# Multi-query attention beside a gated MLP on one core: scores, exponentials and P·V replaced by key moments of third order, under a new list scheduler

## The chip, the cores and the metric

The kernel runs on one core of a Trainium2 chip. The core has a matrix engine (PE, with weight loads listed as PEld), a vector engine (DVE), a scalar engine (ACT), a general engine (POOL), and a sync engine (SP) that mostly issues DMAs; 16 DMA engines move data. Matrix results land in PSUM, eight banks of 128 x 512 float32. Every engine executes its own instruction stream strictly in order and waits on semaphores that other engines raise. The metric is device time of one launch in microseconds, as the median of several runs; a profile is one execution with its own span.

## The reference

```
x = A_x                                    # 2048 x 512, bf16
g = sigmoid((x * gate_w).sum(-1))
q = (x @ wq) -> 32 heads of 16;  k = x @ wk;  v = x @ wv      # one k and v for all heads
p = softmax(q k^T / 4);  a = (p v, heads joined) @ wo
z = gelu(x @ w_in)                         # 2048 x 1376, two halves of 688
z2 = layernorm(second half);  gg = w_sp @ z2 + b_sp           # w_sp is 2048 x 2048
b = (first half * gg) @ w_out
out = g * a + (1 - g) * b
```

All inputs are normal numbers times 0.1 (w_sp times a further 0.01). The scores are small: worked out from the reference's own inputs in float32, the largest |q|² of a head is 2.934, the largest |k/4|² is 0.1369, and the largest score is 0.383.

## The kernel before

Attention is done in 32 units, each 512 queries (one of four chunks) times four heads. For a unit there are 16 key tiles x 4 heads = 64 score blocks of 128 keys by 512 queries. PE makes them (`s_mm`, `ps<-QA,KA`; every matmul goes through the helper at line 394 with a tile position, so that four matmuls on 32 rows or 32 columns of the array run side by side; four such are called a quad below). The blocks are then divided between two ways to exp:

- ACT takes the exp of two or three blocks at a time out of PSUM into a ring `P` (`exp_op`, line 830).
- DVE takes other blocks through a range-checked polynomial: line 842 reads PSUM and writes a linear form into `UW`, line 850 squares it, line 856 squares it again, on DVE or on POOL. The constant and linear rests of the polynomial come back as sums over keys (`SVB`, `KTV`).

PE multiplies the results with `V` into bank 7 (`ps<-P,V` and `ps<-UW,V`). A column of ones in `V` gives the denominators; DVE transposes the unit's result (line 868), and POOL normalises it. The check of the range (`good`, line 920) ends in a flag; were it set, a general path would do all of it again after the fast one.

Beside that run the projections (`xT,wqd`), the second half of z with its normalisation (lines 646 to 670), the first half (lines 639 and 1431), the product with w_sp (`ps<-wT,z`, 24 groups of 17 quads, times the first half at line 714), and the output products (`wo,OT` and `wout,z`, lines 788 and 790).

The order of the instructions on every engine is written by a planner in the build (`pe_step`, `act_step`, `dve_step`, `pool_step`), which keeps a clock per engine with written-out costs. It also puts in products with zeros, `ps<-CT,zer`, where PE's recent share of work in its plan falls below a set value. SP's queue carries few transfers: transposing loads of x, `wT<-in_B_w_sp` in four rounds of four, the weights and the outputs.

Of the kernel before, what the change touches and what calls it, by code (L numbers as in the profile page):

```python
# [2 lines left out]

# [4 lines left out]
ALU = mybir.AluOpType  # L8
# [51 lines left out]
ZP = ()  # L60
W_WIN = 3400.0
W_GEL = 0.98
PR = dict(HALF=100.0, IDR=10, IDN=4, WRES=18, D_HG=3600.0, D_FL=False, WIN=1000.0, WIH=560.0, BACK=32, PRESS=4, FLEX=5000.0, RMIN=48, WBL=0.4, W_MIN=0.9, TTR=50.0, PMX=4, WMX=900.0, PTO=6000.0, PSL=80.0, WP0=45000.0, WG=0, HOLD=0.0, RLEND=0, BMH=2600.0, FST=0.0, TFE=740000.0, PMG=100.0, PLR=130.0)
SCHED = {}
HINT = dict(pe=200, act=40, dve=110, pool=40)
NCHK = 16
L_PE = 235.0
L_X = 40.0
D_END = 110.0
D_DEP = 117.0  # L70
C_SW = 103.0
INFO = None

# [15 lines left out]
class Prog:  # L89

    ENG = ("pe", "act", "dve", "pool", "sp")

    def __init__(self, name):
        self.name = name
        self.ops = {e: [] for e in self.ENG}
        self.lastw = {}
        self.readers = {}
        self.ndma = 0  # L100
# [1934 lines left out]
```

## Time and profile before

| what | value |
|---|---|
| median of 3 runs | 721.99 us (721.9 to 722.15) |
| profiled execution, span | 719.4 us |
| PE busy, matmuls | 700.0 us, 8732 |
| DVE busy, instructions | 702.9 us, 992 |
| ACT busy, instructions | 702.3 us, 752 |
| POOL busy, instructions | 533.9 us, 463 |
| exps on ACT (line 830) | 677.1 us |
| DMA moved | 20.04 MB, mean 28 GB/s |

The median of the runs is 2.6 us above the profile's span; the span is from the first to the last instruction of one execution. Busy time on PE counts a matmul until its modelled end, so that two pipelined matmuls overlap in it; how far apart matmuls start says more. The granted PE clock is shown as a share of full speed.

### The profile page before, as it was taken

The page shows a single profiled execution, that of the slowest core. Times are in us where ns is not written, and L with a number is a line of the kernel's source. Part 1 is how long each engine was busy: PE and PEld are TensorE (multiplying, and loading weights), DVE is VectorE, ACT ScalarE, POOL GpSimd, SP SyncE. Part 2 cuts the span into 40 slices and gives each one's busy share as a digit, 9 for nine tenths or more (in the row PEclk, how much of TensorE's full clock was granted, in tenths as well). Part 3 has the DMA queues.
Part 4 walks back from the last instruction along what each step waited for, and adds up shares of the span by engine and source line. Part 5 has one row for each costly group of instructions (what it writes and reads, how often), then busy time and mean ns, then how long its engine had stood idle before and what let it go on. Part 6 is the DMA issues. An engine that isn't in the chain of part 4 may idle for free. (4 is left out here: it accounts for less than half of the span.)

```text
span 719.4 us, 21284 instructions
## 1 busy us (share of the span) xinstructions
PE 700.0 (97%) x8732; PEld 205.8 (29%) x8732; DVE 702.9 (98%) x992; ACT 702.3 (98%) x752; POOL 533.9 (74%) x463
## 2 busy tenths in 40 slices
PE   8999999999999999999999999999999999999997
PEld 3322223322522222222222322222322222223222
DVE  5999999999999999999999999999999999999997
ACT  5999999999999999999999999999999999999995
POOL 5358877877546857888777888787887787777882
PEclk9999999999999999999999999999999999999999
DMA  8334000000001000510002340000052000000000
GB/s 162 110 94 89 2 1 2 2 3 1 3 1 31 2 1 2 104 43 4 3 1 39 61 81 9 3 1 2 2 118 31 1 17 17 1 2 2 18 14 32
DMA packets 59804, 20.04 MB, mean 28 GB/s; under 512 B 54804, under 2 KB 59192, under 8 KB 59704
## 3 DMA queue, kind: packets, MB, share of 16 engines
q1 hardware_dynamic: 57448, 18.36, 12.1%
q8 instruction: 69, 1.13, 0.7%
q10 hardware_dynamic: 2256, 0.30, 0.3%
q14 instruction: 31, 0.25, 0.1%
HBM read 3.38 MB, written 2.10 MB: 8 GB/s over the span
## 5 line engine op out<-in xcount | busy, mean ns | idle before, releaser
L830 ACT ACTIVATE P<-ps 128x1024 bf16<-128x1024 f32 (+1 forms) x732 | 677.1, 1104 | 2.4 <-PE ps L394 1.8
L856 POOL TENSOR_TENSOR UW<-UW 128x512 f16<-128x512 f16 (+3 forms) x341 | 441.3, 1294 | 128.9 <-DVE UW L842 44.3
L842 DVE TENSOR_SCALAR UW<-ps 128x512 f16<-128x512 f32 (+1 forms) x433 | 359.2, 853 | 3.4 <-PE ps L394 1.8
L394 PE MATMUL ps<-QA,KA 32*128 32x512 bf16 x2048 | 316.3, 384 | 11.2 <-ACT P L830 5.1
L394 PE MATMUL ps<-P,V 128*32 128x512 bf16 x1472 | 184.9, 386 | 0.4 <-DVE KN L563 0.2
L850 DVE TENSOR_TENSOR UW<-UW 128x2048 f16<-128x2048 f16 (+1 forms) x154 | 179.4, 1165 | 0.4
L394 PEld LDWEIGHTS ps<-QA,KA 32*128 32x128 bf16 x2048 | 82.4, 91 | 303.3 <-ACT P L830 146.6
L394 PE MATMUL ps<-wT,z 128*32 128x512 bf16 (+1 forms) x1536 | 111.5, 366 | 0.0
L394 PE MATMUL ps<-UW,V 128*32 128x512 f16 x576 | 108.1, 384 | 0.3
L856 DVE TENSOR_TENSOR UW<-UW 128x1024 f16<-128x1024 f16 (+6 forms) x147 | 96.6, 671 | 0.0
L394 PEld LDWEIGHTS ps<-P,V 128*32 128x32 bf16 x1472 | 43.5, 94 | 61.6 <-issue 57.9
L394 PEld LDWEIGHTS ps<-wT,z 128*32 128x32 bf16 x1536 | 27.8, 94 | 43.3 <-issue 40.0
L394 PE MATMUL ps<-CT,zer 128*32 128x512 bf16 x416 | 37.1, 383 | 0.0
L539 POOL TENSOR_TENSOR QSQ<-QA 128x512 bf16<-128x512 bf16 x16 | 24.8, 1552 | 13.8 <-DVE UW L842 5.7
L394 PEld LDWEIGHTS ps<-UW,V 128*32 128x32 bf16 x576 | 25.4, 94 | 19.0 <-issue 12.0
L394 PE MATMUL ps<-wout,z 128*32 128x512 bf16 x384 | 30.3, 384 | 0.1
L394 PE MATMUL ps<-win,xT 128*32 128x344 bf16 x512 | 29.5, 313 | 0.2 <-DVE z L646 0.2
L868 DVE STREAM_TRANSPOSE T<-ps 128x512 f32<-128x512 f32 (+1 forms) x33 | 22.6, 688 | 0.7 <-PE ps L394 0.7
L394 PE MATMUL ps<-CT,SVB 128*32 128x512 bf16 x128 | 22.8, 383 | 0.0
L394 PE MATMUL ps<-xT,win 128*32 128x512 bf16 (+1 forms) x384 | 22.1, 363 | 0.1
L394 PE MATMUL ps<-xT,wqd 128*32 128x512 bf16 x256 | 21.9, 386 | 0.1
L896 POOL TENSOR_TENSOR win<-T,rc 128x512 bf16<-128x512 f32 x11 | 17.6, 1600 | 3.9 <-DVE UW L856 2.6
(111 smaller groups left out, 329.3 us busy)
## 6 DMA issues: line engine op xcount, KB each, us to landing
out_dram<-outsb SPq DMA_DIRECT2D x15, 128.0 KB, 1.9
win<-in_B_w_in_dram SPq DMA_DIRECT2D x1, 1376.0 KB, 6.3
wout<-in_B_w_out_dram SPq DMA_DIRECT2D x1, 640.0 KB, 4.1
wo<-in_A_wo_dram SPq DMA_DIRECT2D x8, 64.0 KB, 2.4
KA<-KA SPq DMA_DIRECT2D x4, 112.0 KB, 2.4
UW<-in_A_wq_dram SPq DMA_DIRECT2D x1, 384.0 KB, 4.1
wT<-in_B_w_sp_dram SPq DMA_TRANSPOSE x16, 4.5
UW<-in_A_wq_dram ACTq DMA_DIRECT2D x1, 128.0 KB, 3.9
```

The costliest lines, as they stand in the source:

```text
L394: return t.matmul(dst, lhsT, rhs, start=start, stop=stop, tile_position=tp)
L539: dq(pl_q, 1050.0, lambda: op("pool", lambda v: v.tensor_tensor(QSQ[:, q % 2, :], QA[:, q % NQ, :], QA[:, q % NQ, :], ALU.mult), r=[("Q", ...
L830: op("act", lambda a: a.activation(P[:, 512 * p0:512 * (p0 + n)], ps[:, 512 * b0:512 * (b0 + n)], ACT.Exp), r=[bkey(b0 + i_) for i_ in ran ...
L842: op("dve", lambda v: v.tensor_scalar(UW[:, s, 512 * i:512 * (i + n)], bank(b, 512 * n), Q_A, Q_AS, ALU.mult, ALU.add), r=[bkey(b + j) for ...
L850: op("dve", lambda v: v.tensor_tensor(src, src, src, ALU.mult), r=k, w=k, tag="dTT")
L856: op(eng, lambda v: v.tensor_tensor(src, src, src, ALU.mult), r=[("U", s, h) for h in range(a // 2, (b + 1) // 2)], w=w, after=after, tag= ...
L868: return lambda: pgx.op("dve", lambda v: v.transpose(T1[:, jj, c0:c1], bank(BO, c1 - c0, c0)), r=[bkey(BO)], w=[("T1", jj, c0)], tag="T1")
L896: pgx.op(eng, lambda v: v.tensor_tensor(dst, t1v[:, j0:j1, b0:b1, 0:16], rc[:, j0:j1, b0:b1].unsqueeze(3).broadcast_to([128, n, nb, 16]), ...
```

## The change

The scores are no longer formed. Exp is replaced by a cubic, C0 + C1 s + C2 s² + C3 s³, valid for |s| up to 0.655. Since s is a product of q and k, sums over keys can be taken first:

- **Moments (once).** From k and v the kernel forms sums over all 2048 keys of v, k, k kᵀ (as pairs), and of pair products of k times k and times v (`K3`, `T`; lines 549 to 588). The pairs are k_r k_(r+i) for r = 0..15 and i = 0..7, so 128 rows; i = 8 is handled apart (`E`, `kkE`).
- **Pair products of queries.** Work goes in 16 units of 512 queries x 8 heads, each in two halves of four heads. `Qt` is written to DRAM (`qe`, line 618; eight wrapped rows are copied behind it, line 620) and read back in two layouts: `Y` repeats each dimension r eight times, `YB` gives dimension r+i (lines 628 and 630, 512 KB each), and `E` reads pairs for i = 8. `X = Y * YB` is 128 x 512 per head (line 658, on DVE or POOL, as the planner chose).
- **Meeting the moments.** For every head two quads make `W = T3ᵀ X`, 256 x 512, in a pair of banks, (0,1) or (2,3). DVE multiplies both by the query (`Pr`, line 665, 128 x 1024 out of PSUM), and a quad with a 0/1 matrix (`Pr,cs`) sums over the dimension into the numerator bank 4. Lower orders are added there by `T1b`, `TEb`, `M2`; the denominators are gathered in bank 5 (`T2b`, `T3d`), and DVE finishes them at line 680.
- **Per 512 queries (line 691 on).** Denominators of four units are joined, inverted, spread by 0/1 products (`Rh,sg`), and line 702 writes the normalised heads into `OT`, which lies in the buffer of `win`.
- **The MLP** is the same mathematics. Both gelus now read PSUM on ACT (lines 712, 738), with quads as before.
- **The range check** compares max |q|² · max |k/4|² with 0.655² / 1.016 = 0.4223; the flag leads to a general path that computes scores, maxima and exps.
- **The planner** is new: a list scheduler (`Plan.run`) over tasks with costs and priorities; it deals out banks (0 to 3 for `W` while it lasts, 4 and 5 for a unit's sums, 6 and 7 for the rest) and takes for each engine the ready task of lowest priority number. It has no filling with zeros; 11 warming matmuls of 128 columns stand at the start.

Cut to its core, the diff is:

```diff
-        def s_mm(dst_bank, blk, key):
-            u, kt, g = blk
-            e = u % 2
-            kr = ["K0a" if kt == 4 * XO[0] else ("K0", kt // 4)] if e == 0 else [("K1", kt // 4)]
-            mm(bank(dst_bank), KA[32 * g:32 * g + 32, e, 128 * kt:128 * kt + 128], QA[32 * g:32 * g + 32, (u // 2) % NQ, :], True, True,
-               kr + [("Q", (u // 2) % NQ)], [key], tp=(32 * g, 0), chan="s", tag="S")
...
-            op("act", lambda a: a.activation(P[:, 512 * p0:512 * (p0 + n)], ps[:, 512 * b0:512 * (b0 + n)], ACT.Exp),
-               r=[bkey(b0 + i_) for i_ in range(n)], w=[("P", p0 + i_) for i_ in range(n)], tag="exp")
...
-            op("dve", lambda v: v.tensor_scalar(UW[:, s, 512 * i:512 * (i + n)], bank(b, 512 * n), Q_A, Q_AS, ALU.mult, ALU.add),
...
+        def g_q(u):
+            tg, G = u // 4, u % 4
+            s = u % NQT
+            g = Group("any")
...
+            add({"act": (520.0, lambda a: a.activation(Qt[:, s, :], bank(g.b), ACT.Copy))}, 0, None, w=[("Q", s)], grp=g, evac=True, pri=1, tag="Qev")
+            o0 = 24 * 4096 * u
+
+            def wr(q):
+                return [q.dma_start(dap(qe, o0 + 512 * j, [[2048, 2], [4096, 16], [1, 512]]), Qt[32 * j:32 * j + 32, s, :]) for j in range(4)]
...
+            load("sp", lambda q: q.dma_start(Y[:, n % NY, :, :].rearrange("p j n -> p (j n)"), dap(qe, o0, [[4096, 16], [0, 8], [1, 2048]])), [("Y", n % NY)], r=[("qe", u)],
+                 size=524288, pri=10 + u + 0.1 * e, chan="y%d" % (n % NY), tag="Y")
...
+                    xf = lambda v, xi=xi, j=j, n=n: v.tensor_tensor(X[:, xi, :], Y[:, n % NY, j, :], YB[:, n % NYB, j, :], ALU.mult)
+                    add({"pool": (1350.0, xf), "dve": (370.0, xf)}, 0, None,
+                        r=[("Y", n % NY), ("YB", n % NYB)], w=[("X", xi)], pri=pr_, tag="X")
+                    gw = Group("W", 2)
+                    for t in range(2):
+                        add("pe", c_mm(512), mm4(lambda gw=gw, t=t: gw.b + t, 512, 0, T3[:, t, :], X[:, xi, :], True, True),
+                            r=["T3", ("X", xi)], grp=gw, pri=pr_, tag="W")
+                    add("dve", 1150.0, lambda v, gw=gw, pi=pi, n=n, j=j: v.tensor_tensor(Pr[:, pi, :, :], bank(gw.b, 1024).rearrange("p (t n) -> p t n", t=2),
+                                                                                      Y[:, n % NY, j, :].unsqueeze(1).broadcast_to([128, 2, 512]), ALU.mult),
+                        r=[("Y", n % NY)], w=[("Pr", pi)], grp=gw, evac=True, pri=5, tag="Pr")
...
+        def allowed(g, plan):
+            k = g.banks
+            if k == "W":
+                return (0, 2)
+            if k in ("N", "T"):
+                return (4,)
+            if k in ("D", "K3"):
+                return (5,)
...
+        add("dve", 80.0, lambda v: v.tensor_scalar(qk1[0:32, 5:6], qk1[0:32, 2:3], S_MAX * S_MAX / SLACK, None, ALU.is_le), r=["qk2"], w=["qk4"], pri=30, tag="guard")
```

How the streams change is best seen in three places. SP's queue at the start, first before, then now (`L301` and `L507` load x, `L618` writes `Qt` to DRAM, `L620` copies the wrapped rows, `L628` and `L630` load `Y` and `YB`):

```order
L301 DMA_TRANSPOSE xT<-in_A_x_dram 128x4x512 x2
L305 DMA UW<-in_A_wq_dram 128x4x384
L301 DMA_TRANSPOSE xT<-in_A_x_dram 128x4x512 x2
L313 DMA KA<-KA 112x512 x3
L319 DMA win<-in_B_w_in_dram 128x4x1376
```

```order
L507 DMA_TRANSPOSE xT<-in_A_x_dram 128x4x512 x4
L618 DMA qe<-Qt 2x16x512 x16
L620 DMA qe<-qe 16x2048
L628 DMA Y<-qe 128x1x2048
L644 DMA E<-qe 128x512
L628 DMA Y<-qe 128x1x2048
L620 DMA qe<-qe 16x2048
L630 DMA YB<-qe 128x1x2048
```

Sixteen small writes now stand between the loads of x and the first `Y` and `YB`, where three copies of keys stood.

DVE in the middle of attention, first before, then now (`Pr` is the product out of a bank pair, `X` the pair product, `z` at `L767` the MLP's gating, `win` at `L702` the buffer that holds `OT`):

```order
L842 TENSOR_SCALAR UW<-ps 128x1024
L856 TENSOR_TENSOR UW<-UW 128x768
L850 TENSOR_TENSOR UW<-UW 128x2048
L842 TENSOR_SCALAR UW<-ps 128x1024
L856 TENSOR_TENSOR UW<-UW 128x1024
```

```order
L658 TENSOR_TENSOR X<-Y,YB 128x512 x2
L702 SCALAR_TENSOR_TENSOR win<-Ns,S,ps 128x512
L665 TENSOR_TENSOR Pr<-ps,Y 128x1024
L702 SCALAR_TENSOR_TENSOR win<-Ns,S,ps 128x512
L680 SCALAR_TENSOR_TENSOR Prd<-ps,T1d,Qt 128x512
L767 TENSOR_TENSOR z<-ps,z 128x512
L702 SCALAR_TENSOR_TENSOR win<-Ns,S,ps 128x512
L665 TENSOR_TENSOR Pr<-ps,Y 128x1024
```

Most of DVE's work still comes out of PSUM, but between two `Pr` stand single pieces of other work.

PE near its end (`Prd,cs` joins the last denominators, `wT,z` is the product with w_sp, `wo,win` and `wout,z` the output products):

```order
L469 MATMUL ps<-X,T 32x512 x8
L728 MATMUL ps<-wT,z 32x256 x32
L469 MATMUL ps<-bspz,ones 32x512 x4
L469 MATMUL ps<-wT,z 32x512 x12
L476 MATMUL ps<-Prd,cs 32x128 x16
L469 MATMUL ps<-wT,z 32x512 x16
L476 MATMUL ps<-Pr,cs 32x512 x8
L469 MATMUL ps<-wo,win 32x512 x16
L469 MATMUL ps<-wout,z 32x512 x8
```

```order
L469 MATMUL ps<-bspz,ones 32x512 x4
L469 MATMUL ps<-wT,z 32x512 x16
L469 MATMUL ps<-wout,z 32x512 x16
L469 MATMUL ps<-wT,z 32x512 x48
L728 MATMUL ps<-bspz,ones 32x256 x4
L728 MATMUL ps<-wT,z 32x256 x36
L469 MATMUL ps<-wout,z 32x512 x16
L728 MATMUL ps<-wT,z 32x256 x28
L469 MATMUL ps<-wout,z 32x512 x16
```

The last `W` is the first row of the first piece; behind the last denominators, PE still has most of the fourth round of the w_sp product and eight output tiles, and the second piece ends its stream. Before, that work stood among score blocks.

By count of these streams the changed kernel's PE issues 1076 quads of 512 columns, 128 of 344, 84 of 256, 16 of 288, 176 of 128 columns and 112 smaller; DVE some 380 instructions, of them 128 `Pr` and 42 `X`; POOL 86 `X` and 16 `E`; ACT 120 activations; SP 221 transfers.

More of the change, by code (lines that the diff above doesn't have):

```diff
@@ L287, in build_kernel, with diag, mm4, f @@
-        dprev = [None]
-        def sp_dma(fn, r=(), w=(), n=16, chain=True, tag=""):
-            o = op("sp", fn, r=r, w=w, dma=n, after=[dprev[0]] if chain and dprev[0] is not None else [], tag=tag)
-            dprev[0] = o
-            return o
+        def diag(t):
+            a = t[:, :, :]
+            return bass.AP(tensor=a.tensor, offset=a.offset, ap=[a.ap[0], [48, 2], [1, 16]])
+        pl = Plan()
+        pl.bank_last = [None] * 8
+        add = pl.add
+        def mm4(b, n, off, lhsT, rhs, start, stop):
+            def f(t):
+                return [t.matmul(ps[32 * q:32 * q + 32, 512 * b() + off:512 * b() + off + n], lhsT[:, 32 * q:32 * q + 32], rhs,
+                                 start=start, stop=stop, tile_position=(0, 32 * q)) for q in range(4)]
+            return f
@@ L294, in nonc, with load @@
+        def load(eng, fn, w, r=(), size=0, n=1, pri=0.0, chan=None, rate=DMA_RATE, tag="", after=()):
+            if chan is None:
+                chan = "d%d" % nd[0]
+                nd[0] += 1
+            return add(eng, 2600.0 if rate < DMA_RATE else 540.0 * n, fn, r=r, w=w, dma=16 * n, size=size, pri=pri, chan=chan, rate=rate, tag=tag, after=after)
         def nonc(fn):
@@ new lines, in build_kernel @@
+        gw_ = Group("any")
+        for _ in range(WARM):
+            add("pe", 430.0, lambda t: t.matmul(bank(gw_.b, 128), ones[:], ones[:], start=True, stop=True), r=["ones"], grp=gw_, pri=-1, tag="warm")
+        add("dve", 100.0, lambda v: v.tensor_copy(qk1[:, 7:8], bank(gw_.b, 1)), w=["junk"], grp=gw_, evac=True, pri=0)
+        for c in range(4):
+            load("sp", lambda q, c=c: q.dma_start_transpose(xT[:, :, 512 * c:512 * c + 512], x2[512 * c:512 * c + 512, :]), [("x", c)],
+                 size=524288, pri=c, rate=187.0, tag="x")
@@ L724, in put_out @@
[L724 to L725 removed]
+                return [t.matmul(ps[32 * q:32 * q + 32, 512 * b() + off:512 * b() + off + 256], lhsT[:, 32 * (q % 2):32 * (q % 2) + 32], rhs[:, 256 * (q // 2):256 * (q // 2) + 256],
+                                 start=start, stop=stop, tile_position=(0, 32 * q)) for q in range(4)]
+            return f
@@ L1012, in build_kernel @@
-        st_ = {"ua": 0, "kf": 0, "ke": 0, "pu": 0, "gate": False, "mode": "P", "nact": None, "run": 0}
-        stepb = {}
-        sdone = {}
-        estart = {}
-        eend = {-1: 0.0, -2: 0.0}
-        pbusy_ = [False] * PB
-        pfree_ = [0.0] * PB
-        ppos = [0]
-        def p_alloc(n, now):
-            p0 = ppos[0] if ppos[0] + n <= PB else 0
-            if any(pbusy_[i] or pfree_[i] > now for i in range(p0, p0 + n)):
-                return None
-            return p0
-        pr = dict(PR, **SCHED.get(0, {}))
@@ new lines, in build_kernel @@
+        first_w = [t for t in pl.tasks if t.tag == "mom"][0]
+        def allowed(g, plan):
[6 more added lines that the diff above has]
+                return (5,)
+            wide = first_w.eng is None or last_w.eng is not None
+            if k == "L":
+                return (0, 1, 2, 3) if last_w.eng is not None else ()
+            if k == "any" and wide:
+                return (6, 7, 0, 1, 2, 3)
+            return (6, 7)
```

2387 lines of the change are left out of this document (754 added, 1633 removed).

## The prediction

> **What bounds the kernel now.** First the page's busy shares and the costliest groups.
>
> ```profile
> span 719.4 us, 21284 instructions
> PE 700.0 (97%) x8732; PEld 205.8 (29%) x8732; DVE 702.9 (98%) x992; ACT 702.3 (98%) x752; POOL 533.9 (74%) x463
> ```
>
> ACT and DVE are both full; the groups kept apart by shape say with what:
>
> ```profile
> L830 ACT ACTIVATE P<-ps 128x1024 bf16<-128x1024 f32 x722 | 665.9, 1100 | 1.4 <-PE ps L394 0.9
> L842 DVE TENSOR_SCALAR UW<-ps 128x512 f16<-128x512 f32 x290 | 187.2, 677 | 2.9 <-PE ps L394 1.4
> L842 DVE TENSOR_SCALAR UW<-ps 128x1024 f16<-128x1024 f32 x143 | 173.1, 1211 | 0.6 <-PE ps L394 0.4
> ```
>
> ACT spends 666 us of 719 on exps of two score blocks, and idles 1.4 us before them. DVE takes the blocks that ACT cannot. So the number of scores to put through exp on two engines sets the time. That work goes away altogether; what bounds the new kernel has to be built up from its parts.
>
> **What one piece of work costs.** The start-to-start distance in a dense stretch is the price, since neighbours overlap. From the timeline:
>
> ```profile
> 404.67 1.21 DVE L842 TENSOR_SCALAR UW<-ps 128x1024 f16<-128x1024 f32 x1
> 405.80 0.67 DVE L856 TENSOR_TENSOR UW<-UW 128x1024 f16<-128x1024 f16 x1
> 406.40 0.68 DVE L535 CAST QA<-ps 128x512 bf16<-128x512 f32 x1
> 407.00 1.27 DVE L842 TENSOR_SCALAR UW<-ps 128x512 f16<-128x512 f32 x2
> 403.21 0.40 DVE L714 TENSOR_TENSOR z<-ps,z 112x256 bf16<-112x256 f32 x1
> 403.55 1.20 DVE L850 TENSOR_TENSOR UW<-UW 128x2048 f16<-128x2048 f16 x1
> ```
>
> 1024 columns out of PSUM take 1.13 us (404.67 to 405.80), 512 take 0.60, and 256 with a second tensor from SBUF 0.34: the second tensor adds nothing, so a `Pr` costs 1.13 when dense. Each DVE instruction is 0.07 to 0.08 us cheaper than its own duration. If overlap fails because every `Pr` waits for PE, the price is the whole 1.21.
>
> ```profile
> 185.23 3.41 PE L394 MATMUL ps<-xT,win 128*32 128x512 bf16 x60
> 11.58 0.70 PE L394 MATMUL ps<-wvg,xT 128*32 128x33 bf16 x64
> ```
>
> 60 matmuls are 15 quads: (3.41 - 0.38) / 14 = 0.216 us per quad of 512 columns, 0.38 being the length of one (3.41 us covers 15 starts and one end). 16 small quads take 0.70 us, 0.044 each. Other widths lie between in proportion: 0.146 for 344 columns, 0.109 for 256, 0.12 for 288, 0.056 for 128.
>
> **PE.** 1076 x 0.216 = 232.8; 128 x 0.146 = 18.7; 84 x 0.109 = 9.2; 16 x 0.12 = 2.0; 176 x 0.056 = 9.9; 112 x 0.044 = 4.9; together 277.5 us. Along PE's stream 22.6 us of this stands ahead of the first `W`, 216 from there to the last denominators, 39 behind them.
>
> **DVE.** Durations from these rows, less 0.075 each:
>
> ```profile
> L856 DVE TENSOR_TENSOR UW<-UW 128x512 f16<-128x512 f16 x17 | 7.0, 412 | 0.0
> L714 DVE TENSOR_TENSOR z<-ps,z 128x512 bf16<-128x512 f32 x20 | 13.5, 677 | 0.0
> L760 DVE SCALAR_TENSOR_TENSOR outsb<-ps,G,z 128x512 bf16<-128x512 f32 x2 | 1.4, 748 | 0.2 <-PE ps L394 0.2
> L660 DVE BATCH_NORM_STATS2 bst<-z 128x6 f32<-128x344 bf16 x32 | 13.8, 495 | 0.0
> L670 DVE TENSOR_SCALAR z<-z,mv,rstd 128x688 bf16<-128x688 bf16 x16 | 8.0, 568 | 0.0
> L517 DVE TENSOR_REDUCE km<-ps 128x1 f32<-128x512 f32 x4 | 2.7, 666 | 0.0
> L881 DVE RECIPROCAL rc<-T 128x32 f32<-128x32 f32 x15 | 5.0, 330 | 0.0
> ```
>
> 128 `Pr` x 1.136 = 145.4; 42 `X` x 0.337 = 14.2; 32 at lines 680 and 702 x 0.673 = 21.5; 20 gatings x 0.602 = 12.0; 32 statistics x 0.42 = 13.4; 16 normalisations x 0.493 = 7.9; 16 maxima of 128 columns at 0.2 = 3.2 (from the 512-column reduction, 384 columns less); four inversions of 128 columns at 1.05 (330 ns at 32, eight ns per further column) and their neighbours, 7; moments, projections' copies and the rest some 17. Together about 241 us; by full durations 269. Some 21 us stand ahead of the first `Pr`, 210 between it and the last denominators, 9 behind.
>
> So neither engine is clear of the other: between first `W` and last denominators PE has 216 us, DVE 210 (232 if nothing overlaps). Taking the eight stretches of 16 `W` and the larger of the two in each gives 219. PE has the last word, since 39 us of its work stand behind the last denominators, where DVE has 9.
>
> **ACT and POOL** fall out of the bound. ACT: 120 activations at 0.59 us or less:
>
> ```profile
> L830 ACT ACTIVATE P<-ps 128x512 bf16<-128x512 f32 x1 | 0.6, 592 | 0.0
> 18.32 1.22 DVE L842 TENSOR_SCALAR UW<-ps 128x1024 f16<-128x1024 f32 x1
> 18.48 1.04 POOL L539 TENSOR_TENSOR QSQ<-QA 128x512 bf16<-128x512 bf16 x1 [2.31 <-DVE UW L850]
> L539 POOL TENSOR_TENSOR QSQ<-QA 128x512 bf16<-128x512 bf16 x16 | 24.8, 1552 | 13.8 <-DVE UW L842 5.7
> ```
>
> about 71 us with four table loads. POOL: 106 products, 1.04 us beside a DVE that reads PSUM, 1.55 in the mean of the old mix; 110 to 165 us, hidden under 216.
>
> **The start.**
>
> ```profile
> 0.72 5.04 SPq L301 DMA_TRANSPOSE xT<-in_A_x_dram  x2
> 32.51 5.04 SPq L325 DMA_DIRECT2D wo<-in_A_wo_dram  x8
> wout<-in_B_w_out_dram SPq DMA_DIRECT2D x1, 640.0 KB, 4.1
> xT<-in_A_x_dram SPq DMA_TRANSPOSE x4, 5.5
> ```
>
> SP issues a transposing load in 2.52 us and a plain one in 0.63. Four of the first end at 10.8; sixteen writes of `Qt` take 10.1 more, to 20.9; six further issues bring the first `YB` to 24.7, and it lands 4.1 us from its issue (the 640 KB row; these are 512 KB), at 28. One product on DVE later, PE can start `W` at about 29. The moments are not later: the last chunk of x is issued at 8.3 and lands 5.5 later, at 14 (at 17 if the weights slow it), and projection, pair products, the sums and their copies add some 6 to 8 us on DVE. PE itself has 22.6 us of work from 6.2 on, part of it at a cold clock, which also ends near 29. I take 29.
>
> **The end.**
>
> ```profile
> 713.62 0.82 PE L394 MATMUL ps<-win 128*32 128x512 bf16 x11
> 714.27 1.26 ACT L788 ACTIVATE outsb<-ps,G 128x512 bf16<-128x512 f32 x2 [4.24 <-PE ps L394]
> 714.62 2.29 SPq L725 DMA_DIRECT2D out_dram<-outsb  x3
> ```
>
> From PE's last end (714.4) to the end of the span (719.4) are 5.0 us: two evictions, the store, its landing. The new end is the same.
>
> **The sum.** 29 to the first `W`, 255 of PE's work from there, 5.0 at the end: 289 with PE never waiting. Waits between the two nearly equal engines are not in any row. They cost nothing if one always hides the other; 3 if only the eight stretches count (219 for 216); 16 if DVE's full durations pace the middle (232 for 216); and 11 where a `W` stands behind a stretch of about 5 us of other work, which the stream has four times (a fifth, of 12.6 us, falls where DVE has the statistics to do), while DVE has at most two `Pr` in hand (2.3 us): 4 x 2.7 = 11. I take 13, between the last two. That is a span of 302, and with 2.6 for what the median (721.99) has over the span, **305 us**; the forecast's own range is 294 to 325. Against 722 it is 417 us less.
>
> **Cover that could fail.** The traffic is new: a unit loads 2.1 MB of `Y` and `YB`, 0.26 of `E`, moves 0.2 through `qe` and 0.13 out, and has on average one transposing load of w_sp.
>
> ```profile
> 21.00:24.00 3.00, 2.92 (x89) 1.50 (x84) 3.00 (x5) 3.00 (x5) 1.66 (x2) 1.00 1.01 400
> 48.00:66.00 18.00, 17.66 (x209) 5.16 (x208) 17.90 (x26) 18.00 (x20) 14.47 (x12) 1.00 0.56 117
> ```
>
> (The last three columns are granted clock, share of the DMA engines, GB/s.) The load of `win` went at 400 GB/s; the four transposing loads of w_sp kept the engines 0.56 x 18 = 10.1 us, 2.5 each. A unit then needs 2.69 / 0.4 + 2.5 = 9.2 us of DMA against 216 / 16 = 13.5 on PE: hidden, with a third to spare. SP issues some 13 transfers per unit, about 10 us: hidden too, but in one queue, in which a `Y` stands behind waits of `Qt` writes and w_sp loads.
>
> **Rivals.**
>
> *DMA paces the middle (17 in 100).* If rows of 1 and 4 KB out of DRAM go at half the rate of `win`, a unit needs 13.4 + 2.5 = 16 us: 16 x 16 = 256 for 216, so with half the forecast's waits 302 + 40 - 6 + 2.6, about **340 us**. For it: no row shows reads of written DRAM. Against: 400 GB/s with rows of 2.75 KB. It decides once a unit's DMA is over 13.5 us. The Trainium skill, page "DMA: Bandwidth & Descriptors", section "Why a DMA increments its semaphore by 16 and not by 1", says that a transfer uses as many engines as divide both slowest dimensions; the `Qt` writes, whose slowest dimension is 2, would use two, and no run here shows such a transfer. By its 27 GiB/s per engine I estimate 2.3 us more per unit on those two: not over 13.5 by itself.
>
> *The clock falls (9 in 100).* The new planner does not fill PE's gaps, and
>
> ```profile
> 9.00:12.00 3.00, 2.25 (x94) 1.02 (x82) 0.49 (x3) 2.94 (x3) 1.78 (x5) 1.00 1.37 237
> 716.00:718.00 2.00, 0.00 (x0) 0.00 (x0) 0.00 (x0) 0.00 (x0) 0.00 (x0) 0.63 0.58 193
> ```
>
> PE at 2.25 of 3 us keeps clock 1.00; without work it falls to 0.63 and then lower. If a quarter of PE's clock is lost from the first `W` on, 255 becomes 340, and the waits vanish in it: 29 + 340 + 5 + 3 = **377 us**. It decides where PE's share falls well under three quarters; the sum gives 277.5 of 302. The Trainium skill, "TensorE: Matmul & The Clock Gate", section "A second HAM failure mode: psum-queue depth-cycling", speaks against this change: PE that idles briefly between groups while it cycles through PSUM banks can drop to half clock again and again. The trace agrees only that idleness drops it, here to 0.63.
>
> *The range check says no (2 in 100): slower than before.* Then the general path follows the fast one: 32 passes of 16 key tiles, each with two exps of 1024 (1.10 us each by line 830) and, in a first sweep, maxima over 2048 columns (2.26 by twice 1.13): 32 x 16 x 4.46 = 2284 us, about **2,590 us** in all. It decides at 0.4223; the inputs give 2.934 x 0.1369 = 0.4017, five per cent under, more than bf16 rounding of squares takes. This is also the case in which the change doesn't do what it says.
>
> *The forecast: 72 in 100.*
>
> **How the numbers follow.** Within 0.2% of 722 (about what a measurement of this kernel can tell from no change) no case falls; only the refused range check is slower. Faster 0.98, same 0, slower 0.02. The range for 8 in 10 reaches from the forecast's low end past its high end into the DMA case: 294 to 345. The clock case is left out.
>
> **What would show it.** Right: PE and DVE both at 80 to 92% busy with neither ACT nor POOL above 60%; the first `W` at 27 to 31 us; some 40 us from the last denominators to the end with DVE nearly idle; `Pr` at 1.1 to 1.2 us; the chain of waits mostly PE. Wrong: `Pr` over 1.3 us, or starts of quads over 0.23 us; the first `W` after 35; idle time before `X` put down to `Y` or `YB` (DMA); a granted clock under 0.95 (clock gate); a busy ACT behind the end (general path).

## The result and the profile after

The changed kernel takes **344.2 us** in the median of five runs (342.3 to 350.3) against 721.9 before: a ratio of 0.4752, 95% interval 0.474 to 0.4763. The forecast was 305 us with a range of 294 to 345. The time lies just inside the range's upper end, 39 us above the point.

The profiled execution of the changed kernel is one of its slower ones (span 348.4 us, granted clock 0.973 over the span; the other four spans were 340.5 to 345.8). First the heads of the page and the groups that the prediction priced:

```profile
span 348.4 us, 14091 instructions
PE 300.0 (86%) x6381; PEld 165.7 (48%) x6381; DVE 267.8 (77%) x381; ACT 69.5 (20%) x124; POOL 132.8 (38%) x125
L665 DVE TENSOR_TENSOR Pr<-ps,Y 128x1024 bf16<-128x1024 f32 x128 | 150.9, 1213 | 8.8 <-PE ps L469 7.2
L658 POOL TENSOR_TENSOR X<-Y,YB 128x512 bf16<-128x512 bf16 x86 | 101.1, 1176 | 100.3 <-DMA YB<-qe 57.5
L658 DVE TENSOR_TENSOR X<-Y,YB 128x512 bf16<-128x512 bf16 x42 | 29.3, 736 | 5.1 <-DMA YB<-qe 3.2
YB<-qe SPq DMA_DIRECT2D x32, 512.0 KB, 6.7
```

PE is busy for 86% of the span and DVE for 77%; neither ACT nor POOL comes near the bound. The price of a `Pr` is as forecast. Three rows are not: an `X` on DVE takes 0.736 us where 0.412 was taken, POOL waits 57.5 us for `YB`, and a load of `YB` lands 6.7 us after its issue instead of 4.1.

The span in three stretches, cut at the first `W` and at the last denominators (the start of line 691's last instruction). The columns are length, busy time of PE, PEld, DVE, ACT and POOL, granted clock, share of the DMA engines and GB/s:

```profile
0.00:50.38 50.38, 30.14 (x927) 20.56 (x931) 27.27 (x67) 17.45 (x31) 15.77 (x25) 0.89 0.79 169
50.38:304.00 253.62, 231.17 (x4623) 123.22 (x4618) 230.34 (x299) 47.39 (x87) 117.07 (x101) 0.99 0.89 192
304.00:348.40 44.40, 38.73 (x840) 21.93 (x832) 10.22 (x18) 4.62 (x7) 0.00 (x0) 0.98 0.09 28
```

The forecast had 29, 229 (216 of work and 13 of waits) and 44 (39 and 5.0). So the start is 21 us longer, the middle 25, and the end is right. In the middle the DMA engines are taken for 0.89 of the time, which the forecast put at two thirds (9.2 of 13.5 us).

The chain of waits, in order of time, shows what a late `YB` does there (start, length, what; this chain reaches back to 135 us):

```profile
150.24 5.43 DMA YB<-qe
...
167.83 4.84 SPq L746
...
172.78 0.53 SPq L628
...
173.41 7.26 DMA YB<-qe
...
250.03 6.72 DMA YB<-qe
```

Three times the chain leaves PE and DVE and runs through a load of `YB`; at 167.83 SP's transposing load of w_sp (line 746) stands in front of it as well. And the start, by the timeline:

```profile
0.73 19.91 SPq L507 DMA_TRANSPOSE xT<-in_A_x_dram  x4
20.69 10.05 SPq L618 DMA_DIRECT2D qe<-Qt  x16
34.28 0.51 SPq L630 DMA_DIRECT2D YB<-qe  x1
40.29 1.15 PE L469 MATMUL ps<-wT 128*32 128x288 bf16 x15 [3.58 <-issue]
41.55 0.42 DVE L574 TENSOR_TENSOR T<-ps,cf 128x256 bf16<-128x256 f32 x1 [3.87 <-PE ps L469]
42.94 1.01 POOL L719 TENSOR_TENSOR rstd<-ve,nhalf 128x4 f32<-128x4 f32 x1 [8.26 <-DVE ve L718]
44.01 4.29 DVE L722 TENSOR_SCALAR z<-z,mv,rstd 128x688 bf16<-128x688 bf16 x4
44.19 1.29 POOL L658 TENSOR_TENSOR X<-Y,YB 128x512 bf16<-128x512 bf16 x1 [0.23 <-POOL rstd L719]
48.98 1.62 PE L469 MATMUL ps<-win,xT 128*32 128x344 bf16 x20 [4.50 <-DVE qm L816]
50.38 1.92 PE L469 MATMUL ps<-X,T 128*32 128x512 bf16 x16
52.17 1.12 DVE L603 TENSOR_SCALAR G<-gs 128x16 f32<-128x16 f32 x1
```

The loads of x keep SP until 20.6 us, not 10.8. The sixteen writes of `Qt` then take the 10.1 us that were forecast. The third moment is written at 41.6 (`T`, line 574), and 9 us pass from there to the first `W`: one group of PE waits for `qm`, which stands on DVE behind four normalisations of 1.07 us each.

### The profile page after: what moved, and what is told of

Same layout as the page of the kernel before. It is cut to its first block, busy times and chain, and to the rows that moved or that the text cites. A ratio compares the mean times of both kernels' runs of the same rounds, so it can differ in the third digit from the quotient of the medians.

```text
span 348.4 us, 14091 instructions
## 1 busy us (share of the span) xinstructions
PE 300.0 (86%) x6381; PEld 165.7 (48%) x6381; DVE 267.8 (77%) x381; ACT 69.5 (20%) x124; POOL 132.8 (38%) x125
## 4 chain that ended last, share of the span: by engine, by line
PE 39%; DVE 9%; DMA 6%; issue 3%; SPq 2%; POOL 1%; DVEq 0%; POOLq 0%
PE ps L469 32%; DMA YB<-qe 6%; PE ps L476 4%; DVE Pr L665 4%; DVE X L658 3%; PE ps L728 2%; SPq L746 1%; POOL X L658 1%; DVE win L702 1%; DVE Prd L680 0%; DVE outsb L794 0%; SPq L628 0%; DVE Rf L692 0%; DVE Rf L693 0%; SPq L796 0%
## 5 line engine op out<-in xcount | busy, mean ns | idle before, releaser
L665 DVE TENSOR_TENSOR Pr<-ps,Y 128x1024 bf16<-128x1024 f32 x128 | 150.9, 1213 | 8.8 <-PE ps L469 7.2
L658 POOL TENSOR_TENSOR X<-Y,YB 128x512 bf16<-128x512 bf16 x86 | 101.1, 1176 | 100.3 <-DMA YB<-qe 57.5
L469 PE MATMUL ps<-X,T 128*32 128x512 bf16 x1024 | 83.4, 388 | 11.3 <-issue 3.7
L469 PE MATMUL ps<-wT,z 128*32 128x512 bf16 x1280 | 88.5, 380 | 2.2 <-issue 2.2
L469 PEld LDWEIGHTS ps<-X,T 128*32 128x32 bf16 x1024 | 28.3, 97 | 40.9 <-DVE Pr L665 12.8
L767 DVE TENSOR_TENSOR z<-ps,z 128x512 bf16<-128x512 f32 x20 | 13.6, 680 | 29.1 <-PE ps L469 29.1
L658 DVE TENSOR_TENSOR X<-Y,YB 128x512 bf16<-128x512 bf16 x42 | 29.3, 736 | 5.1 <-DMA YB<-qe 3.2
L646 POOL TENSOR_TENSOR E<-E 128x512 bf16<-128x512 bf16 x16 | 18.5, 1158 | 22.7 <-DMA E<-qe 21.2
L476 PE MATMUL ps<-Pr,cs 128*32 128x512 bf16 x256 | 21.6, 388 | 2.0 <-DVE Pr L665 1.9
L714 DVE BATCH_NORM_STATS2 bst<-z 128x6 f32<-128x344 bf16 x32 | 15.1, 493 | 9.1 <-ACT z L712 9.1
L469 PE MATMUL ps<-xT,win 128*32 128x512 bf16 x320 | 20.8, 380 | 0.0
L469 PE MATMUL ps<-xT,wq 128*32 128x512 bf16 x256 | 18.5, 398 | 0.7 <-DMA wq<-in_A_wq_dram 0.5
L702 DVE SCALAR_TENSOR_TENSOR win<-Ns,S,ps 128x512 bf16<-128x512 f32 x16 | 11.7, 741 | 6.8 <-PE ps L469 6.2
```

The costliest lines, as they stand in the source:

```text
L469: return [t.matmul(ps[32 * q:32 * q + 32, 512 * b() + off:512 * b() + off + n], lhsT[:, 32 * q:32 * q + 32], rhs, start=start, stop=stop, ...
L476: return [t.matmul(ps[32 * q:32 * q + 32, 512 * b() + off:512 * b() + off + n], lhsTs[q], rhss[q], start=start, stop=stop, tile_position=( ...
L646: add("pool", 1350.0, lambda v: v.tensor_tensor(E[:, 1, u % 2, :], E[:, 1, u % 2, :], E[:, 0, u % 2, :], ALU.mult), r=[("E", 0, u % 2)], w ...
L658: xf = lambda v, xi=xi, j=j, n=n: v.tensor_tensor(X[:, xi, :], Y[:, n % NY, j, :], YB[:, n % NYB, j, :], ALU.mult)
L665: add("dve", 1150.0, lambda v, gw=gw, pi=pi, n=n, j=j: v.tensor_tensor(Pr[:, pi, :, :], bank(gw.b, 1024).rearrange("p (t n) -> p t n", t=2 ...
L702: add("dve", 640.0, lambda v, gr=gr, u=u, G=G: v.scalar_tensor_tensor(OT[:, tg % 2, G, :], Ns[:, u % NNS, :], S0[:, 0:1], bank(gr.b), ALU. ...
```

## The experiments

Two measures are used. The times are medians, with the ratio to the kernel before on the same chip. From each profile, the middle stretch is compared with the PE work that lies in it. The changed kernel has 216 us of dense work there, with 4623 matmul records; where another order puts n more records into the stretch, n / 4 quads of 0.216 us are added. What the stretch is longer than that is called the **excess**. It is 253.6 - 216 = 37.6 us for the changed kernel; the forecast said 13.

| kernel | us | ratio (95%) | first `W` | middle | excess | DMA share |
|---|---|---|---|---|---|---|
| changed | 344.2 | 0.4752 (0.474–0.4763) | 50.4 | 253.6 | 37.6 | 0.89 |
| quarter of `Y`, `YB` | 332.4 | 0.4608 (0.4588–0.4628) | 48.9 | 236.4 | 20.3 | 0.49 |
| all `X` on POOL | 344.2 | 0.4729 (0.4691–0.4767) | 51.6 | 258.5 | 31.8 | 0.85 |
| both of these | 324.5 | 0.4488 (0.4474–0.4501) | 51.9 | 240.5 | 13.7 | 0.48 |
| rows of w_sp | 342.3 | 0.4741 (0.4723–0.4759) | 47.8 | 243.2 | 27.3 | 0.76 |
| third `YB` buffer | 347.0 | 0.4767 (0.475–0.4784) | 49.3 | 243.7 | 37.7 | 0.92 |
| planner's prices | 347.9 | 0.4831 (0.4804–0.4858) | 49.5 | 272.0 | 36.6 | 0.83 |

Each kernel's runs spread over 1 to 3.5%, so differences under 1% between two of them are not told apart.

The planner's order and the bytes of the changed kernel were profiled three more times, with small edits that come below: with even rows for the writes of `Qt`, with another distance between the rows of `qe`, and with three things moved in the start. The middles of the first and the last:

```profile
45.73:298.90 253.17, 231.05 (x4625) 123.03 (x4618) 228.87 (x299) 47.36 (x87) 120.17 (x104) 0.98 0.90 194
46.75:299.20 252.45, 230.48 (x4623) 123.15 (x4618) 228.22 (x303) 47.39 (x87) 119.52 (x103) 0.99 0.90 194
```

With the other distance the middle is 251.0 us, from 52.1 on. So the middle repeats to 3 us and the end to 0.4 (44.4 to 44.8); what differs between these four profiles, with spans from 343.7 to 348.4, is the start: 45.7 to 52.1 us.

### A quarter of the transfers

```diff
-dma_start(Y[:, n % NY, :, :]..., dap(qe, o0, [[4096, 16], [0, 8], [1, 2048]]))
+dma_start(Y[:, n % NY, 0, :], dap(qe, o0, [[4096, 16], [0, 8], [1, 512]]))
-dma_start(YB[:, n % NYB, :, :]..., dap(qe, o0, [[4096, 16], [4096, 8], [1, 2048]]))
+dma_start(YB[:, n % NYB, 0, :], dap(qe, o0, [[4096, 16], [4096, 8], [1, 512]]))
```

with block 0 read in place of block j by `X` and `Pr`.

> Y and YB are loaded with a quarter of their columns, and all four blocks of a product pass read that quarter, so the pair products are wrong; every instruction of every engine stays in its place. Theory T (the transfers are late): between first W and last denominators the changed kernel took 253 us for 216 us of PE's work, and the transfers kept all 16 DMA engines at 0.89 there; with 1.5 MB less per unit the stretch falls by at least 20 us, to about 230, and the time to 318 to 324 us; the waits of POOL's X for YB (57 us) nearly vanish and YB lands in under 4 us instead of 6.7. Rival C (two nearly equal engines and ports, DVE busy for 230 of the 253 us): the stretch stays within 6 us of 253, and the time at 337 to 342 us, whatever the transfers do.

Measured 332.4 us. The stretches, as above:

```profile
48.91:285.30 236.39, 228.28 (x4625) 115.48 (x4618) 225.37 (x299) 47.47 (x87) 116.58 (x101) 0.99 0.49 108
285.30:329.70 44.40, 38.72 (x840) 20.24 (x832) 10.21 (x18) 4.61 (x7) 0.00 (x0) 0.96 0.09 28
```

Every instruction of the four engines is in its old place, and the middle is 17 us shorter. So 17 of the 25 us that the middle has too much go with the transfers' bytes (15 to 17, against the four middles of 251 to 254). The rest is something else: now DVE is busy for 225 of 236 us. Both theories held a part, and the time lies between them. The medians differ by 12 us, less than the two profiles. `YB` lands in 3.9 us instead of 6.7, as theory T said, but the waits for it did not nearly vanish:

```profile
POOL X L658 <- DMA YB<-qe: 33.0, 12, 6.5
```

The transposing loads of w_sp also held SP's queue for 2.8 us each instead of 5.0 (medians). How much of the 17 us came through that queue, and how much through the landing of `Y` and `YB` themselves, was not told apart.

The two rows also give the price. The engines were taken for 0.89 x 253.6 = 226 us before and 0.49 x 236.4 = 116 now, for 23.2 MB less (192 GB/s x 253.6 us against 108 x 236.4; it is three quarters of the 59 loads of 512 KB that are issued in the stretch). I estimate from it some 210 GB/s, where the forecast took 400 from the load of `win`. (The expectations below reckon with 230, and from it 317, because all 64 loads were counted.) A unit then takes about 226 / 16 = 14.1 us of all engines; the forecast had 9.2, and PE needs 13.5.

### All X on POOL, alone and with the quarter

```diff
-add({"pool": (1350.0, xf), "dve": (370.0, xf)}, 0, None,
+add({"pool": (1350.0, xf)}, 0, None,
```

> All 128 products X go to POOL; before 42 of them were on DVE at 0.74 us each (0.41 in the kernel before the change). The planner sets the rest anew. Rival C (DVE, busy 230 of 253 us, paces the middle): 29 us less on DVE, and the time falls by 10 to 20 us. Theory T (late transfers pace it): POOL has 170 us of work in 253 and waits for YB all the same; within 4 us, and rather slower, since a late block can no longer be made up at DVE's speed.

Alone it took 344.2 us, no different from the changed kernel. Its middle, and that of the second kernel, which has both edits:

> Both earlier edits together: a quarter of the columns of Y and YB (products wrong, as before) and all X on POOL. With the quarter alone the stretch from first W to last denominators fell from 253 to 236 us, and DVE was busy for 225 of the 236; with X on POOL alone it stayed at 259. Theory (two causes that each hide the other: the transfers pace the changed kernel, and with light transfers DVE does, its X beside POOL's products at 0.74 us each): DVE then has some 200 us of work, PE is the bound, the stretch comes to within 8 us of PE's dense work in it (216 to 228, by how much of the feed-forward lies in it), and the time falls below the quarter's alone by 5 to 12 us, to 320 to 328. Rival (what is left over PE's 216 us is PE's own: banks, fetches, clock): within 3 us of the quarter's 332.4.

```profile
51.56:310.10 258.54, 241.53 (x4822) 124.91 (x4814) 205.15 (x254) 50.52 (x91) 164.13 (x142) 0.98 0.85 189
```

```profile
51.94:292.40 240.46, 234.76 (x4822) 120.33 (x4814) 203.68 (x254) 50.41 (x91) 164.04 (x142) 0.99 0.48 106
```

With both, 324.5 us, some 8 less than the quarter alone. DVE's load is 204 to 205 us in both kernels; in this pair, relieving it pays only where the transfers are light. The stretch is longer in them than in their neighbours because 10.7 us of the feed-forward work moved into it out of the end (4822 records for 4623; the end is 32.7 us instead of 44.4).

The excess tells it in one line: 37.6, 31.8 with `X` on POOL, 20.3 with light transfers, 13.7 with both. Transfers cost 17 to 18 us in either pair, and `X` on DVE some 6. The medians are less even: light transfers take off 12 us with `X` shared and 20 with `X` on POOL, and `X` on POOL takes off nothing beside the full transfers and 8 us beside the light ones. The start, which the excess leaves out, may be part of it: its length varies by 6 us in one and the same order. What remains, 13.7 us, has the size of the waits between PE and DVE in the forecast. But PE is idle for only 5.7 us of this stretch (240.46 less 234.76), and the waits that the profile lists for its matmuls there come to under 5 us. The other 8 lie within matmuls that count as busy, and what spaces them was not found.

### Why an X on DVE is dear

Two profiles hold the same four normalisations, with POOL at work and without. The changed kernel's rows stand above: four in 4.29 us, from 44.01, with POOL at its `X` from 44.19 on. The kernel with 32 even rows for the `Qt` writes (below) happened to have POOL idle there:

```profile
42.09 1.55 DVE L722 TENSOR_SCALAR z<-z,mv,rstd 128x688 bf16<-128x688 bf16 x4
43.47 1.18 POOL L658 TENSOR_TENSOR X<-Y,YB 128x512 bf16<-128x512 bf16 x1 [1.44 <-DMA YB<-qe]
44.45 2.14 DVE L658 TENSOR_TENSOR X<-Y,YB 128x512 bf16<-128x512 bf16 x3
```

Four in 1.55 us without POOL for most of it, and 4.29 beside it. The instruction of line 603, over 16 columns, takes 1.12 us in the changed kernel beside POOL, and 0.16 in the run with moved work, in the gap between two of POOL's products:

```profile
48.82 0.16 DVE L603 TENSOR_SCALAR G<-gs 128x16 f32<-128x16 f32 x1
48.94 1.16 POOL L646 TENSOR_TENSOR E<-E 128x512 bf16<-128x512 bf16 x1 [0.32 <-DMA E<-qe]
```

So an `X`, a normalisation or the instruction of line 603 on DVE lasts as long as the product that POOL has begun; an `X` there takes 0.41 to 1.40 us, 0.74 in the mean. Not every instruction of DVE from SBUF to SBUF does so. The statistics of line 714 keep their 0.46 to 0.52 us in every profile, here between 46.96 and 50.64, while POOL makes three `X`:

```profile
48.23 0.50 DVE L714 BATCH_NORM_STATS2 bst<-z 128x6 f32<-128x344 bf16 x1
```

A `Pr`, with one operand in PSUM, takes 1.16 to 1.23 us throughout. The Trainium skill has the rule, in "SBUF — State Buffer", section "SBUF: two separate sides": the port pair that VectorE and GpSimd share is an exclusive lock, not a division of bandwidth, held for a whole instruction, and VectorE needs it in its two-port modes or with two SBUF inputs. The trace agrees, with 1.07 us for a normalisation beside POOL and 0.39 without; the prediction should have drawn on it.

### Where the transfers' price comes from

Four kernels asked what in the transfers costs. First the writes of `Qt`, for the rule of the Trainium skill that the prediction weighed, by which these writes would use two engines:

```diff
-dap(qe, o0 + 512 * j, [[2048, 2], [4096, 16], [1, 512]])
+dap(qe, o0 + 512 * j, [[2048, 32], [1, 512]])
```

> The writes of Qt go out as 32 evenly spaced rows instead of 2 x 16, with the same bytes and the same issues; the rows of pairs land in another order, so the products are wrong. If writes whose slowest dimension is 2 use two DMA engines, and these two are what the loads of Y and YB behind them wait for: the landing of YB falls from 6.7 us by 1 us or more and the time by 5 to 12 us. If the two engines are not what anything waits for, or the writes are spread anyway: within 1.5 us of the changed kernel.

346.9 us (343.0 to 350.6), no gain, and `YB` lands in 6.7 us as before. How many engines the writes used, no view shows; nothing was seen to wait for them. Next the source of the large loads:

```diff
-Y: dap(qe, o0, [[4096, 16], [0, 8], [1, 2048]])
+Y: dap(wsp_d, 2048 * 128 * (n % 16), [[2048, 128], [1, 2048]])
-YB: dap(qe, o0, [[4096, 16], [4096, 8], [1, 2048]])
+YB: dap(wsp_d, 2048 * 128 * ((n + 8) % 16), [[2048, 128], [1, 2048]])
```

> Y and YB are loaded as 128 different rows of 2048 columns of w_sp, with the same bytes, row length and waits, instead of 16 rows eight times (Y) and 16 overlapping sets of eight rows (YB) of what was written just before; the products are wrong. In the changed kernel these two move about 25 MB in 109 us of all 16 engines, 230 GB/s (from the quarter run's difference). Theory R (repeated reads of the same few rows of DRAM are slow): the rate goes up towards the 400 GB/s of win in the kernel before, the engines' share between first W and last denominators falls from 0.89 to about 0.65, and the time by 6 to 12 us. Rival (rows of 4 KB spread over 128 partitions go at this rate from any source): share and time stay, within 3 us.

```profile
47.79:291.00 243.21, 229.51 (x4622) 116.10 (x4618) 226.54 (x298) 47.37 (x87) 117.59 (x101) 0.99 0.76 200
```

The engines are taken for 0.76 x 243.2 = 185 us instead of 226: 41 us less for the same 59 loads of 512 KB, 30.9 MB. At the estimated 210 GB/s these take 147 us; 41 less is 106 us, or some 290 GB/s. The excess fell by 10 us in this profile, which is the shortest of its four runs. The median fell by 2 us only, inside the spread, so in time it is not decided. By this the different rows went faster than the same rows read eight times; 400 GB/s was not reached by either.

The rows of `qe` lie exactly 8 KB apart. A kernel that computes the same with another distance (the access patterns on `qe` follow; they are left out here):

```diff
-qe = nc.dram_tensor("qe", (16 * 24, 4096), B16).ap()
+qe = nc.dram_tensor("qe", (16 * 24, 4096 + 128), B16).ap()
```

> The rows of qe are 4224 elements apart instead of 4096; everything computed is the same. Y and YB from different rows of w_sp were moved at about 317 GB/s instead of 230, with the engines' share in the middle at 0.76 instead of 0.89. Theory P (it is the distance of exactly 8 KB between the rows that 16 engines read at once): the share falls to about 0.76 as well and YB lands in 5 us instead of 6.7, the time falls by 2 to 8 us. Rival (it is the repeated reading of the same rows, eight times each): share and landing stay, and the time within 3 us.

343.8 us, a ratio of 0.4747 (0.4715 to 0.4779); share 0.88 and landing 6.4 us, as good as unchanged. A distance of 8 KB and 256 bytes is no cure; larger ones were not tried. This leaves the repeated reading as the likelier cause, though the run with w_sp also changed the tensor, and so does not prove it.

Last, a third buffer for `YB`:

```diff
-NY, NYB, NX, NPR, NNS, NPD = 3, 2, 8, 6, 5, 5
+NY, NYB, NX, NPR, NNS, NPD = 3, 3, 8, 6, 5, 5
```

> YB gets a third buffer, as Y has; the planner sets the order anew. If the late YB is a matter of its buffer (the load can be issued only when the products of two blocks before are done): YB is issued a block earlier, POOL's wait for YB falls from 57 us to under 25, and the time falls by 4 to 10 us. If the engines' rate sets it (share 0.89 in the middle, queue never empty): the waits move to another place, and the time stays within 3 us.

347.0 us, and the waits of POOL, which were 57.5 us for `YB`, read

```profile
POOL X L658 <- DMA Y<-qe: 60.3, 18, 6.2
```

The same time is now waited for `Y`, and the excess is 37.7 as before, with the engines taken for 0.92 of the middle. This buffer was not what was short; the share speaks for the engines' rate.

### The planner's prices

```diff
-DMA_RATE = 300.0
+DMA_RATE = 230.0
-add({"pool": (1350.0, xf), "dve": (370.0, xf)}, 0, None,
+add({"pool": (1180.0, xf), "dve": (740.0, xf)}, 0, None,
```

> Only the planner's figures change: 230 GB/s for plain transfers instead of 300, an X at 740 ns on DVE and 1180 on POOL instead of 370 and 1350, all from the profile of the changed kernel. The work is the same, its order and its split between DVE and POOL are set anew. If the order is what is wrong (loads issued late because the plan takes them as quick, and X given to DVE as cheap): 5 to 12 us less. If the transfers' bytes set the pace: within 3 us either way.

347.9 us, not faster; by its interval it is slower by 1 to 2%. The new order moved 420 matmul records out of the end, 359 of them (90 quads, 19 us) into the middle:

```profile
49.53:321.50 271.97, 252.07 (x4982) 133.26 (x4986) 227.52 (x292) 47.85 (x86) 114.92 (x98) 0.99 0.83 185
321.50:341.90 20.40, 15.97 (x420) 8.91 (x408) 8.77 (x15) 3.35 (x5) 0.00 (x0) 1.00 0.09 30
```

The middle is 18 us longer and the end 24 shorter, with an excess of 36.6. More of PE's other work within reach did not fill its waits.

### The start

The first of four kernels that moved the start: `win` is loaded by SP behind x, instead of by ACT beside it.

```diff
-load("act", lambda q: q.dma_start(win[:, :, FH:F], ...), ["win2"], size=704512, pri=-5)
-load("act", lambda q: q.dma_start(win[:, :, 0:FH], ...), ["win1"], size=704512, pri=-4)
+load("sp", lambda q: q.dma_start(win[:, :, FH:F], ...), ["win2"], size=704512, pri=4.5)
+load("sp", lambda q: q.dma_start(win[:, :, 0:FH], ...), ["win1"], size=704512, pri=4.6)
```

> The two loads of win are issued by SP behind the four transposing loads of x instead of by ACT beside them; the planner sets the rest anew. Theory S (the loads beside them slow the transposing loads, 5 us per issue instead of 2.5): the four are issued in about 11 us instead of 20, the writes of Qt end about 8 us earlier, at 23, and the first W comes at 38 to 43 us instead of 50; the time falls by 5 to 9 us. Rival (the transposing loads take 5 us each by themselves in this kernel): still 20 us for four, the writes of Qt later by 1.2 us, and no gain or a loss of up to 3 us.

349.7 us, a ratio of 0.4863 (0.483 to 0.4895): slower.

```profile
0.73 15.14 SPq L507 DMA_TRANSPOSE xT<-in_A_x_dram  x4
17.11 17.00 SPq L618 DMA_DIRECT2D qe<-Qt  x20
34.10 0.41 DVE L574 TENSOR_TENSOR T<-ps,cf 128x256 bf16<-128x256 f32 x1
46.64 0.61 PE L469 MATMUL ps<-X,T 128*32 128x512 bf16 x8
```

The loads of x end at 15.9 instead of 20.6 and the third moment is out at 34.1 instead of 41.6. So the loads beside them did slow the transposing ones, by half of the 10 us that were to be explained. But the first `W` comes at 46.6, within the 45.7 to 52.1 of the old order, since SP is now held until 34 us by twenty writes of `Qt`. The second kernel gave these to ACT as well:

```diff
-load("sp", wr, [("qe", u)], r=[("Q", s)], size=131072, n=4, ...)
+load("act", wr, [("qe", u)], r=[("Q", s)], size=131072, n=4, ...)
```

> win is loaded by SP behind x, as in the earlier run, and all writes of Qt are issued by ACT; the planner sets the rest anew. In the earlier run the moments were out 8 us sooner (34 us against 42), but 20 writes of Qt kept SP until 34 and the first W came only at 46.6. Theory Q (the start has two chains, x to the moments and SP's queue to the first YB, and only shortening both helps): with the queue free of the writes the first YB is issued before 24 us, the first W comes at 36 to 40 us instead of 50, and the time falls by 6 to 12 us against the changed kernel. Rival (behind the moments PE's and DVE's feed-forward work in front of the first W sets it): the first W stays at 44 us or later, and the time within 3 us.

387.0 us, a ratio of 0.5376 (0.5354 to 0.5398). The first `W` comes at 43.0, but:

```profile
42.95:301.40 258.45, 215.38 (x4057) 102.11 (x4053) 223.83 (x292) 48.31 (x92) 130.39 (x113) 0.94 0.81 179
301.40:380.70 79.30, 73.31 (x1540) 41.86 (x1529) 15.25 (x25) 6.77 (x10) 0.00 (x0) 0.98 0.23 50
```

The planner's new order left 700 matmul records more for the end, 79 us instead of 44, and PE was short of work in the middle: 566 records fewer, 185 us of dense work in 258, an excess of 73. The start was a little shorter, and the order lost 43 us. As a test of the start alone this run is spoiled by that.

So the third kernel kept the planner's order and moved three things by hand:

```diff
+qw, qx, Yl, YBl = (ops("sp", k) for k in ("qw", "qx", "Y", "YB"))
+move("sp", [qx[0], Yl[0]], qw[1])
+move("sp", [YBl[0], Yl[1], qx[1], YBl[1]], qw[2])
+move("dve", ops("dve", "z2n")[0:4], ops("dve", "Pr")[3])
+pw = ops("pool", "pow")[0]
...
+move("pool", [pw], ops("pool", "X")[7])
```

> The planner's order of the changed kernel is kept, and three things are moved by hand after it: SP issues the copy and the first loads of Y and YB of units 0 and 1 behind the second and third set of Qt writes instead of behind the fourth; DVE's first four normalisations go behind the fourth Pr; POOL's first power goes behind its eighth X. Nothing is added or left out. Theory Q: the first W stood at 50.4 us because, after the moments (T3 written at 42.3), YB was late (issued at 34.3), POOL's X stood behind the power (to 44.0), and DVE's four normalisations of 1.07 us each beside POOL held the banks for PE. With them out of the way YB is issued at about 29, the first W comes at 43 to 45 us, and the time falls by 3 to 6 us, less than the shift because the moved work is still to be done between the products. Rival (the start is only another place where the same PE and DVE work waits; DVE paces what follows): the first W comes sooner, and the time stays within 1.5 us.

```profile
30.18 0.56 SPq L630 DMA_DIRECT2D YB<-qe  x1
42.13 0.43 DVE L574 TENSOR_TENSOR T<-ps,cf 128x256 bf16<-128x256 f32 x1 [3.18 <-PE ps L469]
46.75 1.92 PE L469 MATMUL ps<-X,T 128*32 128x512 bf16 x16
```

The first `W` comes at 46.8, 3.6 us sooner, with the moments where they were. That alone would prove little, since the first `W` varies by 6 us without any move; but the step from the third moment to it does not vary so. It is 8.8 us in four kernels with this order (the changed one, the quarter, the rows of w_sp and the other distance), 6.1 with the even rows, where POOL was idle beside the normalisations, and 4.6 here. So the moves are worth 4 us of this step. The time is 348.1 us, a ratio of 0.4828 (0.4803 to 0.4852): not faster, rather slower. The middle was 252.5 us and the end 44.5, as in the changed kernel, and the profiled execution was the shortest of its six, at 345.6. Where the others lost what this start gained, no profile shows. The fourth kernel had the same moves with all `X` on POOL:

> The same three moves with all X on POOL. X on POOL alone left the time where it was (ratio to the kernel before 0.4729 against 0.4752), since late transfers pace the middle; with a quarter of the transfers it took 8 us off. If the start's moves are worth 3 to 6 us and X on POOL 1 to 2: 336 to 341 us, better than the changed kernel by 1 to 2 per cent. If the transfers pace all of it: 342 to 345.

344.7 us, 0.477 (0.4748 to 0.4791); the first `W` was at 52.7. Against the third kernel, with the same moves and `X` shared, this is 3 us less, and the two intervals do not meet: here `X` on POOL paid something beside the full transfers, too. No kernel that does the changed kernel's whole work was clearly faster than it.

## Why the prediction was right or wrong

**The shape was right.** The exps are gone, and ACT is no longer the bound (69.5 us for 71 forecast); PE and DVE are, at 86 and 77% (80 to 92 were named, so DVE lies a little under); POOL's 132.8 us lie within 110 to 165. A `Pr` takes 1.21 us alone, a write of `Qt` 0.63, the end behind the last denominators 44.4 for 44. DVE's total is 267.8 us, the forecast's upper sum of 269 by full durations; its lower sum of 241 counted on overlap and on an `X` at 0.337. That the upper sum meets is luck in part: the 42 `X` took 29.3 us of it where 17.3 were counted. That the time lies inside the range is luck in part as well: the upper end of 345 was drawn from the DMA case, and no case held a start that is 21 us longer.

**"29 to the first `W`" failed,** at 50.4. Of the 21 us, 8 begin in the first step: "SP issues a transposing load in 2.52 us". That price is the first two loads of x in the profile before; the next two already took more there (the first row). Here the last of four is issued at 16.7 instead of 8.3 (the second):

```profile
6.45 6.15 SPq L301 DMA_TRANSPOSE xT<-in_A_x_dram  x2
16.74 3.90 SPq L507 DMA_TRANSPOSE xT<-in_A_x_dram  x1
```

With `win` taken from beside them the four took 15.1 us instead of 19.9, so about half of the excess is the loads beside them.

"The moments are not later" failed with it: they come at 42 us where 20 to 25 was argued, partly because of 3.6 us in which PE waited for nothing that the profile shows. And "one product on DVE later" left out what stands in the in-order queues between landing and `W`: a power in front of POOL's `X`, four normalisations on DVE, a group of PE that waits for them. Moving them out was worth 4 us of that step. How the remaining 9 or so divide between the longer landing, PE's stalls and the feed-forward work set into the start was not told apart. A shorter start goes with a shorter span in the four profiles of one order, 45.7 us with 343.7 and 50.4 with 348.4. But in the medians no kernel that was meant to shorten the start gained; what it would take for that stays open.

**"Hidden, with a third to spare" failed.** The term was the 400 GB/s, which a stretch of 3 us with the load of `win` had shown. `Y` and `YB` go at some 210, a unit takes 14.1 us of all engines for 13.5 of PE, and that is over the point which the first rival gave for itself (13.5). Its 16 us per unit were too high, its mechanism was right: 17 us of the middle go with the transfers' bytes. That its time of about 340 came close is luck: its own start was the same wrong 29, and its middle, 256 us and half the waits, some 262, was over the measured 253.6. The sign named for it, idle time before `X` put to `YB`, is the row with 57.5 us.

**"13 of waits"** was too small, because two more things lie in the same stretch: the transfers' 17 us, and some 6 from `X` on DVE at 0.74 us beside POOL. With both away 13.7 us are left. That this meets the 13 is not shown to be more than chance: that kernel's DVE has no `X` to do, PE's idle time there is 5.7 us, and the forecast's own explanation (a `W` behind 5 us of other work, four times) was not tested. The sum by parts: 29 + 21, 229 + 25, 44: 348, the profiled span.

**The clock** did not fall: 0.99 in the middle, 0.89 in the start. The Trainium skill's section on depth-cycling, weighed in the prediction, finds no case here: PE is busy for 231 of 254 us in the middle. **The range check** let the fast path pass.

## What to carry to other kernels

Price a load by a row with the same source pattern: by my estimate, loads that repeat a few DRAM rows went at some 210 GB/s where a plain load had gone at 400, and that turned "hidden" into 17 us of the middle. Before work is shared between DVE and POOL, look which of DVE's SBUF-to-SBUF instructions stretch to the length of POOL's, count them at up to that, and expect little from undoing the sharing while something else is late. One profile's start can differ by 6 us from the next of the same order: compare stretches that repeat before a gain is read from one that does not. When two causes hide each other, take both away in one run: the pair showed 8 us more, where the second alone showed nothing.

## What the runs showed of the hardware

PE stops at fixed places of its stream without a cause in the profile. In the changed kernel, with the quarter of the transfers, and in the last kernel, the waits of PE read, or the timeline shows:

```profile
PE ps L469 <- issue: 16.0, 12, 3.6
```

```profile
PE ps L469 <- issue: 5.3, 5, 1.7
```

```profile
40.63 0.24 PE L469 MATMUL ps<-wkvg,xT 128*32 128x33 bf16 x7 [4.97 <-issue]
```

The stop before the last seven of a group of 64 projections is there in ten of the thirteen profiles of this code: 1.2 to 2.2 us in nine of them, 5.0 in the last kernel. It does not follow the transfers: 1.5 and 1.4 us in the changed kernel and the quarter, 1.4 and 2.0 with all `X` on POOL and with both edits. The sum of such waits is 16.0 us in the changed kernel and 5.3 with light transfers, but 7.9 with the rows of w_sp and 5.9 with the planner's new prices, at full transfers. So it may be a part of the transfers' 17, and that is not shown. Waiting for instructions to be fetched would be one reading; no run here changed the fetches, and the cause stays open.
